# A fused attention, FFN and expert kernel: second products one iteration later, the weight words' intermediate in PSUM, list slots stored without waiting

## The chip, the cores and the metric

The kernel runs on one core of a Trainium2 chip. The metric is the device time of one execution in microseconds (us); a kernel's time is the median over runs. Five engines work side by side and wait for each other through semaphores: PE (TensorE, matrix products), DVE (VectorE), ACT (ScalarE), POOL (GpSimd) and SP (SyncE, which here only issues DMA transfers). Each engine takes its own instructions strictly in order.

## The reference

Three stages follow each other; the second takes the first one's output, the third the second one's.

```
scores = q @ k.T / sqrt(64)                   # 4 batches x 8 heads, 576 x 576
kth    = 32nd largest score of each row
attn   = softmax(scores where scores >= kth)  # the others at -1e9
x      = attn @ v, as 2304 tokens x 512

h = x @ w_in                                  # 512 -> 2048, weights as 8-byte floats
g = maximum(h, 0) + alpha * minimum(h, 0)
x = g @ w_out                                 # 2048 -> 512

logits = x @ w_gate + bias[modality]          # 8 experts
e      = argmax(logits)                       # one expert for each token
out    = softmax(logits)[e] * (relu(x @ w1[e]) @ w2[e])
```

## The kernel before

**Loop.** Attention runs as a software pipeline over 72 iterations (NIT); an iteration takes two tiles of 128 score rows. The order on every engine is the order in which the Python code writes the instructions. In one iteration, for the pair s, DVE finds the 32 largest of each row (L471, L474, L477, L501). PE computes scores for s+1 (L453, L454) and the product with v for s-3 (`av`, L558). ACT copies the scores out of PSUM (L457), makes the mask's operand (L526), the exponentials (L530) and the high half-precision part (L534). POOL subtracts the mask (L527) and makes the low part (L538, L539), and SP issues the transposing DMA PT<-HL (L541).

**FFN within the loop.** As soon as 256 tokens (a chunk) have gone through attention, eight FFN steps for them are fed into the loop, one in an iteration. A step's first product (`mm1`, L637) is issued in one iteration, with a copy by ACT (L651). One iteration later the slope runs on DVE (L665) and the *pair*, that is the high and the low half-precision part of g, on ACT (L672) and POOL (L673). The pair goes into one of GB = 2 buffers named g. In the iteration behind that PE issues the second product (`mm2`, L686), 12 matmuls of 128x512, ahead of the scores and the next `mm1`. PE therefore takes, in an iteration: second product, scores, first product, gate, `av`. The second products of all eight steps add up in two PSUM tiles (psX, two buffers). After the eighth, ACT scales them out (`fin`, L693), PE transposes them back into the same psX (L698), ACT copies these (L700) and PE makes the gate's logits (L704), so the next chunk's first second product waits for L700. What remains behind iteration 72 is done without attention to about 897 us: the *tail*. Then come the experts.

**Weights.** w_in and w_out arrive as 8-byte floats in 32 pieces (L247, 512 KB each, five buffers wraw). `read(x)` turns a piece of 128x512 into f32 by three integer operations on DVE, L259 to L261; their intermediate `t_` is the destination itself, in SBUF: a stretch of Wi or Wo not yet filled, or for the last pieces one of four buffers wlast. ACT and POOL then split the pieces (L266, L271 to L274, L280).

**Lists.** When a chunk's gate is done, `place(r)` writes the tokens' numbers and weights into the experts' lists in DRAM with an indirect DMA on POOL (mapD<-tg,si, L773), with a small memset ahead of it (L772). Only the second place of a chunk is told that it doesn't depend on the first one; all others wait until the earlier places have landed. A block of an expert reads its list back (L1446 for a Block, L1309 for a Unit).

**Stores.** `store()` scales an expert's results into a tile o and writes them out; o has its own buffers in the pools A and B.

Of the kernel before, what the change touches and what calls it, by code (L numbers as in the profile page):

```python
# [8 lines left out]
F32 = mybir.dt.float32  # L9
# [3 lines left out]
I32 = mybir.dt.int32  # L13
I64 = mybir.dt.int64
AF = mybir.ActivationFunctionType
ALU = mybir.AluOpType
# [5 lines left out]
NT, DM, DFF = B * S, H * D, 2048  # L22
E, FE = 8, 1024
KTOP = 32
NCC, NFB = DM // 128, DFF // 128
# [9 lines left out]
LCON = [("late", 1), ("late", 3), ("late", 5)]  # L35
SBUFS = 4
LOOK = 1
GB, GR = 2, 4
ZA, ZN = 1, 1
BIG = 2.0 ** 126  # L40
WBUF = 5
# [19 lines left out]
def tile_kernel(ctx, tc, q, k, v, w_in, w_out, alpha, mod_id, w_gate, mod_bias, w1, w2, out, dbg=None, force=False):  # L61
    nc = tc.nc
    V, A, G, T, SY = nc.vector, nc.scalar, nc.gpsimd, nc.tensor, nc.sync
# [11 lines left out]
    psX = ctx.enter_context(tc.tile_pool(name="psX", bufs=2, space=PSUM))  # L75
# [102 lines left out]
    def phase1(exact, ph, rc, rs, flags, ohs, mp):  # L178
# [51 lines left out]
        def all_weights(words, stage):  # L230
# [20 lines left out]
            def read(x):  # L251

                w_, i = divmod(x, 16)
                f32[x] = W[w_][:, (i + WG) * n:(i + WG + 1) * n] if i + WG < 16 else \
                    stage.tile([128, n], F32, name="wlast", bufs=WG)
                r3 = raws.pop(x).bitcast(I32).rearrange("p (n w) -> p n w", w=2)
                lo, hi = r3[:, :, 0], r3[:, :, 1]
                t_ = f32[x].bitcast(I32)
                V.tensor_scalar(t_, hi, 5, 2, op0=ALU.logical_shift_left, op1=ALU.logical_shift_right)  # L259
                V.scalar_tensor_tensor(t_, hi, -1073741824, t_, op0=ALU.bitwise_and, op1=ALU.bitwise_or)  # L260
                V.scalar_tensor_tensor(t_, lo, 29, t_, op0=ALU.logical_shift_right, op1=ALU.bitwise_or)  # L261

            def square(x):
                w_, i = divmod(x, 16)
# [331 lines left out]
        def chunk(ci, xn, rs):  # L596
# [174 lines left out]
            def place(r):  # L771
                G.memset(spacer, 0.0)  # L772
                d_ = G.indirect_dma_start(out=mapD, out_offset=bass.IndirectOffsetOnAxis(ap=c.si[:, r:r + 1], axis=0),  # L773
                                          in_=c.tg[:, r, :], in_offset=None)
                if r:
                    tc.declare_no_dep(d_.ins, c.placed.ins, reason="other slots")
                c.placed = d_
                state.placed += 1

            def keep():  # L780
# [105 lines left out]
        wgroup = all_weights(words, stage)  # L886
        state.ffn = state.out = None
        state.started = state.placed = 0
        state.alone = False

        def wstep(n):
# [51 lines left out]
        def first_block(s_):  # L943
# [51 lines left out]
            def start():  # L995
                assert state.placed == NTILE - 2
                mp.b0 = Block(0, blk0[0:1, 0:1], blk0[0:1, 1:2], mp)
                for fp in range(4):
                    mp.b0.load(fp)

# [54 lines left out]
        while True:  # L1055
# [44 lines left out]
            for c, fp in post:  # L1100
                for f in c.slope(fp):
                    f()
            for c, fp in paired:
                if c.k == NCH and fp == c.n - 1:
                    mp.b0.mm(0, (0,))
                c.mm2(fp)
                if fp == c.n - 1:
                    c.fin()
                    at("mid", s_, lambda c=c, s_=s_: c.after(s_))
                    at("late", s_, c.keep)  # L1110
            del paired[:]
            for c, fp in post:
                c.pair(fp)
                paired.append((c, fp))
            nxt = []
            if s_ + LOOK < NIT:
                nxt = live[s_ + LOOK] = tile_pair(s_ + LOOK)
# [183 lines left out]
    class Unit:  # L1301


        def __init__(self, i, R, ie, ip, mp):
            self.i, self.R, self.mp = i, R, mp
            self.e = SY.value_load(ie, min_val=0, max_val=E - 1)
            pos = SY.value_load(ip, min_val=0, max_val=E * CAP)
            self.ids = small.tile([128, 4, 2], I32, name="ids4")
            SY.dma_start(self.ids[:, :R], mapD[bass.ds(pos, 128 * R), :].rearrange("(p r) o -> p r o", r=R))  # L1309
            self.raw, self.wp, self.gs = {}, {}, {}  # L1310

        def gather(self):
# [68 lines left out]
                             start=(j == 0 and n == 0), stop=(j == 7 and n == 2))  # L1381

        def store(self):
            o = [p_.tile([128, 2, DM], F32, name="o") for p_ in (self.mp.A, self.mp.B)]
            past = []
            for r in range(self.R):
                A.activation(o[r // 2][:, r % 2, :], self.Y[r], AF.Copy, scale=self.ids.bitcast(F32)[:, r, 1:2])  # L1387
                G.memset(spacer, 0.0)
                d_ = G.indirect_dma_start(out=out, out_offset=bass.IndirectOffsetOnAxis(ap=self.ids[:, r, 0:1], axis=0),  # L1389
                                          in_=o[r // 2][:, r % 2, :], in_offset=None)  # L1390
                for f_ in past:
                    tc.declare_no_dep(d_.ins, f_.ins, reason="other rows")
                past.append(d_)

    def moe_phase(nblk, blk, mp):
# [17 lines left out]
        for i in range(1, nblk):  # L1413
# [21 lines left out]
            o.m2(3)  # L1435
            o.store()

    class Block:


        def __init__(self, i, ie, ip, mp):
            self.i, self.mp = i, mp
            self.e = SY.value_load(ie, min_val=0, max_val=E - 1)
            pos = SY.value_load(ip, min_val=0, max_val=E * CAP)
            self.ids = small.tile([128, 2, 2], I32, name="ids")
            SY.dma_start(self.ids, mapD[bass.ds(pos, 256), :].rearrange("(p r) o -> p r o", r=2))  # L1446
            self.raw, self.wp = {}, {}
            self.gs = {}
            self.Y = None
# [73 lines left out]
                                 start=(fp == 0 and fb == 0 and n == 0), stop=(fp == 3 and fb == 1 and n == 2))  # L1523

        def store(self):
            o = self.half().tile([128, 2, DM], F32, name="o")
            for r in range(2):
                A.activation(o[:, r, :], self.Y[r], AF.Copy, scale=self.ids.bitcast(F32)[:, r, 1:2])
                G.memset(spacer, 0.0)
# [36 lines left out]
```

## Time and profile before

| what | value |
| --- | --- |
| runs | 1156.09 us (median of 3; 1155.61 to 1158.4) |
| the profiled execution's own time | 1153.87 us, of which the trace's span is 1152.2 us |
| granted clock of PE, mean | 0.92 of full speed |
| attention's iterations (first L474 at 39.8, last at 777.5 us) | the iteration is about 8.3 us where DVE has no gap |
| tail of the FFN and first block of the experts | to about 930 us |
| experts' units | about 930 to 1152 us |

The profile names an instruction by its line, its engine and output<-inputs. In a timeline a row gives start, duration, the instruction, its shape, and in square brackets how long the engine was idle before it and what ended that. A row of the waits gives the total, the number of waits and the longest. In a row of a time window the numbers in brackets are counts of instructions; the end of the row is the granted clock of PE, the mean busy share of the DMA engines, and GB/s.

### The profile page before, as it was taken

Reading aid. Unit: us, or ns where it says so; the run is one execution under the profiler, and the core shown is the slowest. Engines: PE = TensorE matmul, PEld = TensorE weight load, DVE = VectorE, ACT = ScalarE, POOL = GpSimd, SP = SyncE. Lnnn points to the kernel's source line nnn. Section 1 sums busy time; section 2 is a strip of 40 time slices with the busy share of each in tenths; the row PEclk is TensorE's granted clock in tenths of the full one; section 3 lists DMA queues with packets and bytes.
Section 4 is the critical chain, followed back from the end, with each engine's and each line's share of the span. In section 5 each row is a group of like instructions: output and inputs, shape, how many; then the busy total and the mean of one; then the engine's idle time right before and its main releaser. Section 6 shows DMA issues by size and latency. Waiting matters only on the chain.

```text
span 1152.2 us, 21482 instructions
## 1 busy us (share of the span) xinstructions
PE 845.0 (73%) x7100; PEld 602.6 (52%) x7100; DVE 823.8 (72%) x2813; ACT 755.2 (66%) x1276; POOL 718.0 (62%) x1106
## 2 busy tenths in 40 slices
PE   0202231347869989878787878989998899999995
PEld 0001121234536557455555555667665778888884
DVE  5788878788889999999888879994326343434342
ACT  6466696898987887878888978795324243342441
POOL 4175496899898898888788999897323220230210
PEclk9999565668899999999989999999999999999998
DMA  8969965586788577586778768765104272543320
GB/s 250 251 171 237 263 145 128 137 180 162 165 202 162 107 184 126 106 177 133 147 148 172 158 138 193 155 128 79 19 19 165 86 262 75 183 135 121 129 92 22
DMA packets 297111, 170.22 MB, mean 148 GB/s; under 512 B 245458, under 2 KB 270034, under 8 KB 296988
## 3 DMA queue, kind: packets, MB, share of 16 engines
q1 hardware_dynamic: 293212, 158.24, 59.0%
q0 software_dynamic: 3776, 10.51, 2.5%
q8 instruction: 57, 0.93, 0.4%
q14 instruction: 66, 0.54, 0.2%
HBM read 81.42 MB, written 25.94 MB: 93 GB/s over the span
## 4 chain that ended last, share of the span: by engine, by line
PE 34%; DVE 23%; POOL 15%; ACT 12%; issue 7%; DMA 6%; SPq 3%; ACTq 0%; POOLq 0%
PE psX L1363 9%; PE psS L1380 9%; PE psX L686 6%; DVE X L501 4%; DVE m L477 4%; PE psS L637 4%; POOL HL L538 4%; POOL S L527 4%; DVE F L477 3%; DMA rawk<-in_k_dram 3%; ACT S L530 2%; POOL qk L419 2%; DVE gr L665 2%; ACT HL L534 2%; PE psH L637 2%
## 5 line engine op out<-in xcount | busy, mean ns | idle before, releaser
L686 PE MATMUL psX<-Wo,g 128*128 128x512 f16 x864 | 218.6, 403 | 53.8 <-POOL g L673 39.6
L527 POOL TENSOR_TENSOR S<-u,S 128x576 f32<-128x576 bf16 x144 | 184.5, 1303 | 47.4 <-ACT u L526 47.2
L637 PEld LDWEIGHTS <-Wi 128*128 128x128 f16 x1920 | 170.8, 99 | 45.7 <-DVE gr L665 14.3
L538 POOL TENSOR_TENSOR HL<-S,HL 128x512 f16<-128x512 f32 x144 | 168.2, 1168 | 20.3 <-ACT HL L534 10.5
L453 PE MATMUL psS<-QK 128*128 128x512 f16 (+1 forms) x160 | 63.7, 436 | 142.6 <-DVE B L471 109.4
L637 PE MATMUL psH<-xT,Wi 128*128 128x256 f16 (+1 forms) x1488 | 158.2, 265 | 12.3 <-DVE gr L665 8.5
L686 PEld LDWEIGHTS <-g 128*128 128x128 f16 x864 | 82.9, 103 | 157.1 <-POOL g L673 49.2
L530 ACT ACTIVATE S<-S,bc,nb 128x576 f32<-128x576 f32 x144 | 124.0, 862 | 40.7 <-POOL S L527 40.7
L453 PEld LDWEIGHTS <-QK 128*128 128x128 f16 (+1 forms) x320 | 32.1, 109 | 203.1 <-DVE B L471 59.5
L1389 POOL DMA_INDIRECT out_dram<-o,ids x18 | 19.9, 1106 | 166.8 <-ACT o L1387 164.0
L477 DVE MAX8 m<-X 128x8 f32<-128x160 f32 x432 | 117.6, 314 | 0.0
L673 POOL TENSOR_TENSOR g<-gr,g 128x512 f16<-128x512 f32 x72 | 84.0, 1166 | 52.6 <-ACT g L672 47.3
L526 ACT ACTIVATE u<-S,bc 128x576 bf16<-128x576 f32 x144 | 103.1, 765 | 15.8 <-POOL bc L506 15.8
L1370 DVE SCALAR_TENSOR_TENSOR gl<-psX,gh 128x512 fp32r<-128x512 f32 (+1 forms) x40 | 25.4, 637 | 115.5 <-ACT gh L1369 110.9
L534 ACT ACTIVATE HL<-S 128x576 f16<-128x576 f32 x144 | 91.3, 680 | 12.9 <-DMA PT<-HL 12.7
L1369 ACT ACTIVATE gh<-psX 128x512 fp32r<-128x512 f32 (+1 forms) x40 | 22.3, 557 | 109.7 <-PE psX L1363 107.9
L457 ACT ACTIVATE S<-psS 128x576 f32<-128x576 f32 x144 | 84.1, 633 | 8.6 <-PE psS L454 8.6
L501 DVE MATCH_REPLACE8 X<-m,X 128x160 f32<-128x160 f32 x288 | 87.0, 310 | 0.0
L558 PE MATMUL bankO<-VV,PT 128*128 128x66 f16 (+1 forms) x2240 | 86.0, 200 | 0.0
L558 PEld LDWEIGHTS <-PT 128*128 128x128 f16 (+1 forms) x2240 | 82.3, 105 | 4.8 <-issue 3.5
L474 DVE SCALAR_TENSOR_TENSOR X<-psS,S 128x288 f32<-128x288 f32 (+1 forms) x144 | 80.8, 603 | 2.5
L672 ACT ACTIVATE g<-gr 128x512 f16<-128x512 f32 x72 | 44.9, 623 | 40.5 <-DVE gr L665 24.1
(290 smaller groups left out, 2098.6 us busy)
## 6 DMA issues: line engine op xcount, KB each, us to landing
raw<-in_moe_w_dram SPq DMA_DIRECT2D x40, 512.0 KB
qkD<-QK SPq DMA_DIRECT2D x16, 576.0 KB
QK<-qkD SPq DMA_DIRECT2D x16, 576.0 KB
wraw<-in_moe_w_in_dram SPq DMA_DIRECT2D x16, 512.0 KB
wraw<-in_moe_w_out_dram SPq DMA_DIRECT2D x16, 512.0 KB
vvD<-VV SPq DMA_DIRECT2D x16, 325.0 KB
VV<-vvD SPq DMA_DIRECT2D x16, 325.0 KB
K<-QK SPq DMA_DIRECT2D x32, 144.0 KB
```

The source lines that it names most:

```text
L477: ops.append(lambda: V.max(o, a_))
L501: ops.append(lambda i_=i_, r=r: V.match_replace(out=dst(i_), in_to_replace=m[:, i_, 8 * r:8 * r + 8], in_values=src(i_) if r == 0 else dst ...
L526: A.activation(u, t.S, AF.Relu, scale=-BIG, bias=t.cut)
L527: G.tensor_tensor(t.S, u, t.S, op=ALU.subtract)
L530: A.activation(t.S, t.S, AF.Exp, scale=t.c.negc, bias=t.b)
L534: A.activation(t.HL.rearrange("p a b -> p (a b)")[:, 0:S], t.S, AF.Copy)
L538: G.tensor_tensor(f[:, 640:1152], t.S[:, 0:512], f[:, 0:512], op=ALU.subtract)
L558: T.matmul(oo, l, r, start=(n_ == 0), stop=(n_ == len(ops) - 1), skip_group_check=True)
L637: T.matmul(h[:, fb, :], Wi[:, 4 * cc + f0 // 512, wh, f0 % 512:f0 % 512 + 128], c.xT[:, :R, xh_, cc, :], start=(n == 0), stop=(n == 11))
L686: T.matmul(c.X2[r], g[:, gh, fb, r * 128:r * 128 + 128], Wo[:, FB * fp + fb, wh, :], start=(fp == 0 and fb == 0 and n == 0), stop=(fp == c ...
L1363: T.matmul(h, w_[:, cc, f0:f0 + 128], x_[:, cc, :], start=(n == 0), stop=(n == 11))
L1380: T.matmul(self.Y[r], g_[:, r * 128:r * 128 + 128], w_[:, j % 2, :], start=(j == 0 and n == 0), stop=(j == 7 and n == 2))
```

## The change

1. **Lag.** A pair made in iteration `s_` is noted with the iteration from which its second product may run: `s_ + 2` in place of `s_ + 1`, and still `s_ + 1` where `s_ + 2` would lie behind the last iteration. In the loop the second product comes ahead of the pair of the same iteration, so up to three pairs live: GB is 3. The loop that issues second products stops behind a chunk's last one. A chunk's `fin`, gate, places and its store x2D move with it.
2. **Intermediate in PSUM.** `t_` is a tile of psX; only the third operation writes SBUF. The two psX tiles are not used by anything else while the weights are read.
3. **Places.** Every place is told that it depends on no earlier one, and every reading of a list waits for all places so far (`behind`).
4. **Stores' slots.** o of Block, and of the Unit's first half, takes a buffer of the tile xth in the same pool.

```
-GB, GR = 2, 4
+GB, GR = 3, 4
...
-                t_ = f32[x].bitcast(I32)
+                t_ = psX.tile([128, n], F32, name="psX").bitcast(I32)
                 V.tensor_scalar(t_, hi, 5, 2, op0=ALU.logical_shift_left, op1=ALU.logical_shift_right)
                 V.scalar_tensor_tensor(t_, hi, -1073741824, t_, op0=ALU.bitwise_and, op1=ALU.bitwise_or)
-                V.scalar_tensor_tensor(t_, lo, 29, t_, op0=ALU.logical_shift_right, op1=ALU.bitwise_or)
+                V.scalar_tensor_tensor(f32[x].bitcast(I32), lo, 29, t_, op0=ALU.logical_shift_right, op1=ALU.bitwise_or)
...
-                if r:
-                    tc.declare_no_dep(d_.ins, c.placed.ins, reason="other slots")
-                c.placed = d_
+                for p_ in state.places:
+                    tc.declare_no_dep(d_.ins, p_.ins, reason="other slots")
+                state.places.append(d_)
...
+                mp.places, mp.seen = state.places, 0
+                behind(mp.b0.list, mp)
...
-            for c, fp in paired:
+            last = False
+            while paired and paired[0][0] <= s_ and not last:
+                _, c, fp = paired.pop(0)
+                last = fp == c.n - 1
                 if c.k == NCH and fp == c.n - 1:
                     mp.b0.mm(0, (0,))
                 c.mm2(fp)
...
-            del paired[:]
             for c, fp in post:
                 c.pair(fp)
-                paired.append((c, fp))
+                paired.append((s_ + (2 if s_ + 2 < NIT else 1), c, fp))
...
-            SY.dma_start(self.ids[:, :R], mapD[bass.ds(pos, 128 * R), :].rearrange("(p r) o -> p r o", r=R))
+            behind(SY.dma_start(self.ids[:, :R], mapD[bass.ds(pos, 128 * R), :].rearrange("(p r) o -> p r o", r=R)), mp)
...
-            o = [p_.tile([128, 2, DM], F32, name="o") for p_ in (self.mp.A, self.mp.B)]
+            o = [self.mp.A.tile([128, NCC, 256], F32, name="xth").rearrange("p (r a) t -> p r (a t)", r=2),
+                 self.mp.B.tile([128, 2, DM], F32, name="o")]
...
+    def behind(list_, mp):
+        for p_ in mp.places[mp.seen:]:
+            tc.add_manual_dep(list_.ins, p_.ins.name, mybir.DependencyInfo(
+                mybir.DependencyClass.Sync, mybir.DependencyReason.DATA), reason="all that was placed")
+        mp.seen = len(mp.places)
...
-            SY.dma_start(self.ids, mapD[bass.ds(pos, 256), :].rearrange("(p r) o -> p r o", r=2))
+            self.list = SY.dma_start(self.ids, mapD[bass.ds(pos, 256), :].rearrange("(p r) o -> p r o", r=2))
+            if i:
+                behind(self.list, mp)
...
-            o = self.half().tile([128, 2, DM], F32, name="o")
+            o = self.half().tile([128, NCC, 256], F32, name="xth").rearrange("p (r a) t -> p r (a t)", r=2)
```

The first place is DVE at one of the pieces that go into the buffers wlast. Before:

```order
L259 TENSOR_SCALAR wlast<-wraw 128x512 [waits DMAHW0_49,Pool_49]
L260 SCALAR_TENSOR_TENSOR wlast<-wraw,wlast 128x512 [waits DVE_49]
L261 SCALAR_TENSOR_TENSOR wlast<-wraw,wlast 128x512 [waits DVE_49]
L259 TENSOR_SCALAR wlast<-wraw 128x512 [waits DMAHW1_49]
L260 SCALAR_TENSOR_TENSOR wlast<-wraw,wlast 128x512 [waits DVE_49]
L261 SCALAR_TENSOR_TENSOR wlast<-wraw,wlast 128x512 [waits DVE_49]
```

And after:

```order
L259 TENSOR_SCALAR psX<-wraw 128x512 [waits DMAHW0_49]
L260 SCALAR_TENSOR_TENSOR psX<-wraw,psX 128x512 [waits DVE_49]
L261 SCALAR_TENSOR_TENSOR wlast<-wraw,psX 128x512 [waits DVE_49,Pool_49]
L259 TENSOR_SCALAR psX<-wraw 128x512 [waits DMAHW1_49]
L260 SCALAR_TENSOR_TENSOR psX<-wraw,psX 128x512 [waits DVE_49]
L261 SCALAR_TENSOR_TENSOR wlast<-wraw,psX 128x512 [waits DVE_49]
```

The number of operations stays; two of three write PSUM, and the wait for POOL, which frees the buffer wlast, has moved from the first to the third.

The second place is ACT at the end of attention, where a chunk's sums come out of the loop (x<-psX is L693, gr<-psX is L700; the last L457 belongs to the last iteration's scores). Before:

```order
L526 ACTIVATE u<-S,bc 128x576 x2
L693 ACTIVATE x_11062<-psX,un 128x512 x2
L672 ACTIVATE g<-gr 128x512
L530 ACTIVATE S<-S,bc,nb_8261 128x576
L457 ACTIVATE S<-psS 128x576 x2
L530 ACTIVATE S<-S,bc,nb_8261 128x576
L651 ACTIVATE gr<-psH 128x512
L534 ACTIVATE HL<-S 128x576 x2
L700 ACTIVATE gr<-psX 128x512 x2
L526 ACTIVATE u<-S,bc 128x576 x2
```

And after:

```order
L526 ACTIVATE u<-S,bc 128x576 x2
L672 ACTIVATE g<-gr 128x512
L530 ACTIVATE S<-S,bc,nb_8277 128x576
L457 ACTIVATE S<-psS 128x576 x2
L530 ACTIVATE S<-S,bc,nb_8277 128x576
L651 ACTIVATE gr<-psH 128x512
L534 ACTIVATE HL<-S 128x576 x2
L526 ACTIVATE u<-S,bc 128x576 x2
L693 ACTIVATE x_11245<-psX,un 128x512 x2
L672 ACTIVATE g<-gr 128x512
L530 ACTIVATE S<-S,bc,nb_8627 128x576 x2
L651 ACTIVATE gr<-psH 128x512
```

Both copies stand one iteration later: L693 behind the last L457, and L700 (the second row behind these, after L534) behind the next iteration's exponentials.

The third place is POOL in the tail, at three places in a row (tg and si, the numbers with their weights and the slots, come from DVE). Before:

```order
L745 COPY tg<-tok 128x2 [waits DMASW4_49,DMASW3_49]
L772 MEMSET spacer 1x1
L773 DMA mapD<-tg,si 18944x2
L772 MEMSET spacer 1x1 [waits Pool_49]
L773 DMA mapD<-tg,si 18944x2 [waits DMASW5_49,DVE_49]
L772 MEMSET spacer 1x1 [waits Pool_49]
L773 DMA mapD<-tg,si 18944x2
L673 TENSOR_TENSOR g<-gr,g 128x512 [waits Activation_49]
```

And after:

```order
L745 COPY tg<-tok 128x2 [waits DMASW4_49,DMASW3_49]
L772 MEMSET spacer 1x1
L773 DMA mapD<-tg,si 18944x2
L772 MEMSET spacer 1x1 [waits Pool_49]
L773 DMA mapD<-tg,si 18944x2 [waits DVE_49]
L772 MEMSET spacer 1x1 [waits Pool_49]
L773 DMA mapD<-tg,si 18944x2
L673 TENSOR_TENSOR g<-gr,g 128x512 [waits Activation_49]
```

The order is the same; the middle place has lost its wait for POOL's own earlier DMA (DMASW5) and keeps the one for DVE.

## Rows read from the trace of the kernel before

**Rows 1.** The page's part 1: busy time, share of the span, instructions.

```profile
PE 845.0 (73%) x7100; PEld 602.6 (52%) x7100; DVE 823.8 (72%) x2813; ACT 755.2 (66%) x1276; POOL 718.0 (62%) x1106
```

**Rows 2.** Time windows: busy time of PE, PEld, DVE, ACT, POOL, then clock, DMA.

```profile
400.00:450.00 50.00, 45.33 (x493) 31.10 (x490) 49.37 (x198) 38.37 (x62) 45.24 (x66) 1.00 0.69 142
...
950.00:1000.00 50.00, 50.00 (x226) 40.81 (x226) 17.83 (x22) 17.02 (x25) 9.08 (x12) 1.00 0.39 128
```

**Rows 3.** DVE's groups by shape, 0 to 250 us; then lines L259, L261: min/median/max ns.

```profile
L261 DVE SCALAR_TENSOR_TENSOR wlast<-wraw,wlast 128x512 int32<-128x512 int32 x8 | 10.4, 1300 | 0.3
...
L259 DVE TENSOR_SCALAR Wo<-wraw 128x512 int32<-128x512 int32 x12 | 7.0, 586 | 3.9 <-DMA wraw<-in_moe_w_out_dram 3.9
...
L259 DVE TENSOR_SCALAR Wi<-wraw x12: 411/420/1505, 9.3 to 55.6; 128x512 int32<-128x512 int32 x12
...
L261 DVE SCALAR_TENSOR_TENSOR Wi<-wraw,Wi x12: 691/692/1646, 10.5 to 56.8; 128x512 int32<-128x512 int32 x12
```

**Rows 4.** Timeline around 20 us, one instruction each of DVE and POOL.

```profile
20.53 1.65 DVE L261 SCALAR_TENSOR_TENSOR Wi<-wraw,Wi 128x512 int32<-128x512 int32 x1
...
19.91 1.72 POOL L419 TENSOR_TENSOR qk<-rawk,qk 128x576 f16<-128x576 f32 x1
```

**Rows 5.** Lines L474 and L1370, DVE with a PSUM operand: min/median/max ns.

```profile
L474 DVE SCALAR_TENSOR_TENSOR X<-psS,S x144: 457/602/749, 40.3 to 777.5; 128x288 f32<-128x288 f32 x72, 128x576 f32<-128x576 f32 x72
...
L1370 DVE SCALAR_TENSOR_TENSOR gl<-psX,gh x40: 408/692/693, 935.0 to 1136.1; 128x512 fp32r<-128x512 f32 x32, 128x256 fp32r<-128x256 f32 x8
```

**Rows 6.** Timelines of DVE, then of POOL, 179 to 202 us.

```profile
179.55 1.36 DVE L259 TENSOR_SCALAR wlast<-wraw 128x512 int32<-128x512 int32 x1 [3.06 <-POOL Wi L280]
180.95 1.67 DVE L260 SCALAR_TENSOR_TENSOR wlast<-wraw,wlast 128x512 int32<-128x512 int32 x1
...
193.70 0.46 DVE L474 SCALAR_TENSOR_TENSOR psS<-psS,S 128x288 f32<-128x288 f32 x1
...
201.78 0.20 POOL L506 TENSOR_TENSOR bc<-m,nb 128x4 f32<-128x4 f32 x1 [10.34 <-DVE wp1k L212]
```

**Rows 7.** Timelines of DVE, then of SP, 55 to 78 us.

```profile
55.61 0.41 DVE L259 TENSOR_SCALAR Wi<-wraw 128x512 int32<-128x512 int32 x1
...
68.10 0.46 DVE L474 SCALAR_TENSOR_TENSOR psS<-psS,S 128x288 f32<-128x288 f32 x1
...
77.57 2.00 SPq L247 DMA_DIRECT2D wraw<-in_moe_w_out_dram  x4
```

**Rows 8.** Waits by engine and line: three of 237 to 350 us, two of 562 to 710 us.

```profile
PE psX L686 <- POOL g L673: 14.8, 5, 5.2
...
ACT gr L651 <- PE psH L637: 1.4, 2, 0.7
...
SPq L541 <- PE bankO L558: 2.6, 1, 2.6
...
PE psX L686 <- POOL g L673: 18.1, 6, 4.9
...
SPq L541 <- PE bankO L558: 3.7, 3, 1.5
```

**Rows 9.** End of attention: timelines of PE and ACT, and the chain that ended last.

```profile
779.30 2.75 PE L686 MATMUL psX<-Wo,g 128*128 128x512 f16 x12 [2.79 <-ACT gr L700]
...
785.26 1.48 ACT L534 ACTIVATE HL<-S 128x576 f16<-128x576 f32 x2
...
806.28 2.59 PE psX L686 x12
```

**Rows 10.** Tail, 860 to 868 us: timelines of POOL, DVE and PE.

```profile
860.17 0.98 POOL L773 DMA_INDIRECT mapD<-tg,si  x1 [0.42 <-issue]
...
864.57 0.97 POOL L773 DMA_INDIRECT mapD<-tg,si  x1 [3.32 <-DVE mx L975]
...
860.22 0.17 DVE L769 RECIPROCAL tg<-sm 128x2 f32<-128x2 f32 x1
...
868.05 2.33 PE L686 MATMUL psX<-Wo,g 128*128 128x512 f16 x10 [3.28 <-POOL g L673]
```

More of the change, by code (lines that the diff above doesn't have):

```diff
@@ L888, in phase1 @@
         state.started = state.placed = 0
+        state.places = []
         state.alone = False
```

## The prediction

> **What bounds the kernel now.** I began with the busy shares of the page [rows 1]: PE 73%, DVE 72%, ACT 66%, POOL 62%, so no engine bounds the whole. The time windows say why [rows 2]. Between 400 and 450 us DVE is busy 49.37 of 50 us: attention in its even stretches hangs on DVE. Between 950 and 1000 us PE is busy 50.00 of 50 us: the experts, and most of the tail before them, hang on PE. Whatever the change does to PE, POOL or ACT inside an even stretch of attention is therefore worth nothing there; it can pay only where DVE has gaps: at the start (to about 240 us, while the weights are read), in the stretches at 237 to 350 and 562 to 710 us, and at the end. So I went on with DVE's groups in the first 250 us, the timelines where weights are read, the waits in the two uneven stretches, the chain of waits at the end of attention, and the places in the tail. DVE's groups show the three operations of a read [rows 3]: nine groups for three destinations, 96 instructions, 80.8 us together, of which the first is 10.4 us (1.30 us each) and the last 7.0 us (0.59 us each).
>
> **Part 1, the intermediate in PSUM.** Nothing is removed: 96 instructions stay 96. What may change is how long one takes. In SBUF an undisturbed L259 takes 0.42 us and an undisturbed L260 or L261 0.69 us, but some take up to 1.5 and 1.65 us [rows 3]. The long ones fall on POOL's long ones: POOL's L419 ran 1.72 us from 19.91, and DVE's L261 1.65 us from 20.53 [rows 4]; the two engines alternate there. With a PSUM operand DVE is not stretched, with POOL busy beside it all through attention: L474's 144 instructions have a maximum of 0.749 us, and L1370, the same kind of operation on 128x512, takes 0.692 us with a maximum of 0.693 [rows 5]. No row shows these three integer operations on PSUM; I price each at 0.69 us, the nearest row in shape. For L259 that is worse than its 0.42 us undisturbed. The bounds: 0.42 us for L259 as before, and above, the 0.84 us at which 96 of them take the 80.8 us of now. At 0.69 us they take 66.4 us: 14.4 us less DVE work, net of what L259 loses.
>
> Against the change speaks the Trainium skill, "VectorE: DVE Perf Modes", section "Why PSUM operands drop a tier": a PSUM operand takes the doubled rate from a 4-byte operation. By that page's formula for PSUM sources (its section on the TRN2 errata) one operation would be an estimated 658 ns, so 63.2 us for the 96 where the rows give 66.4. No row before shows L259 on PSUM.
>
> How much of the 14.4 us lies on the path? Three places.
>
> At 179.55 us four reads run back to back until 193.70 us, 14.15 us, the first after an idle of 3.06 us in which it waited for POOL to free the buffer wlast [rows 6]. In the changed order this wait stands at the third operation, so the first two run in that idle. The other ten take 6.9 us. The reads would end at about 186.4 us, 7.3 us earlier. POOL waits for what DVE does next: it stood 10.34 us until 201.78 us for the maxima that DVE makes behind the reads [rows 6]; with 7.3 us less it still waits 3, so the whole 7.3 us is on the path. ACT and SP, which hang on POOL here, move along.
>
> At 55.61 us four reads take until 68.10 us, 12.5 us [rows 7]; at 0.69 us each 8.3, so 4.2 us less. But the next words are only issued by SP at 77.57 us, 9.5 us behind the last read [rows 7], by a queue that holds other waits. I pass on 1.5 us, between 0 and 4.2.
>
> The rest of the 14.4 us (5.9 us of it is the first place's busy time, 4.2 the second's) is 4.3 us, scattered over stretches in which DVE also waits for the words to arrive (the last of the nine groups shows 3.9 us of that [rows 3]). I count it at nothing: the transfers cover it; without that cover it gains up to 4.3.
>
> Sum of part 1: **-8.8 us**, between -3 (half the first place, no second) and -15.8.
>
> **Part 2, the lag inside attention.** In the two uneven stretches PE waits 14.8 and 18.1 us at L686 for POOL's g, 32.9 us in all [rows 8]. With the pair a whole iteration older that wait should go. But a waiting PE costs only what waits for PE. There ACT waits 1.4 us for the first products, and SP 2.6 and 3.7 us at L541 for the products with v [rows 8]: 7.7 us. Half of it I take as on the path, since POOL and ACT, the other engines of the loop, are late next: **-4 us**, between 0 and -10 (just under a third of the 32.9). In DVE's even stretches it is 0. The third buffer costs only room. SP's store x2D of each chunk comes an iteration later, behind that iteration's loads and transposes; nobody reads it before the experts, and its place would cost only if it delayed L541, by the half microsecond of an issue (four took 2.00 us [rows 7]).
>
> **Part 3, the lag at the end of attention.** PE falls idle here, then becomes the bound: at 779.30 us it has waited 2.79 us for L700 and from then on it does not rest; the tail is a chain of second products of 2.59 us each and first products [rows 9]. With the lag, one second product more is left when attention ends: +2.6 us, if PE then works without a gap. The chunk's boundary moves into the next iteration too: L700 comes behind that iteration's L534 (785.26 to 786.7 us) [rows 9], so with the two copies at about 787.8 us. PE does the older second product in place of waiting from 776.5 us; with that, the next first product (2.6 us each) and under 2.3 us of transposes and products with v it runs dry between 783 and 784. It waits some 4 us there in place of 2.79, and then catches up with two second products in a row: 2.6 + 4 - 2.8 = 3.8. So **+4 us**, between +2.6 and +4.7 (dry at 783).
>
> **Part 4, places.** All waits of L773 are short but one, in the tail. The place at 860.17 us was issued; the next at 864.57 us came after 3.32 us of idle; the row names a DVE operation, but the pairs and slots of that chunk were ready at about 860.4 us (L769 at 860.22) [rows 10]. What the order shows as taken away there, POOL's wait for its own earlier DMA, is the one that fits. Without it the three places and the pair behind them are done at about 864.7 us, and PE, which stood 3.28 us until 868.05 us for that pair [rows 10], need not wait. The tail hangs on PE, so **-3.3 us**, and 0 if it was DVE after all. The lists' readings wait for all places as before: 0. The stores' buffers change owner, and their former readers (first products) are long done: 0.
>
> **Sum:** -8.8 - 4 + 4 - 3.3 = -12.1 us. Against the profiled execution's 1153.87 us that is 1141.8; its own time lies 2.2 us under the median of the runs, so against 1156.09 it is **1144 us**. A measurement here tells about 0.3% (3.5 us) from no change: faster means below 1152.6, slower above 1159.6.
>
> **Rivals.** *The lag opens the whole loop* (chance 0.16). The chain in the uneven stretches goes from POOL's g through PE to ACT and back to POOL; if each wait of PE holds back the next iteration, half of the 32.9 us comes back, -16.5 in place of -4, and the time is 1156.1 - 24.6 = 1131.5. For it: five of those waits are nearly 5 us each [rows 8]. Against: the direct waits for PE are 7.7 us.
>
> *The gains are hidden* (0.15). The words, not DVE, set the start, and POOL's 10.34 us wait shrinks only until ACT's scores are late; part 1 is -3, part 2 is 0, with +4 and -3.3 the time is 1156.1 - 2.3 = 1153.8. For it: the idle times before L259 are put down to the words. Against: at 179 us all words have arrived, the wait there is for POOL.
>
> *The change doesn't shorten the reads* (in the next case): if an operation between SBUF and PSUM is stretched by POOL as before, or takes over 0.84 us, part 1 is 0. Against: the maxima in rows 5; but L261 still reads and writes SBUF besides PSUM.
>
> *The end of attention costs more than the rest gives* (0.07). The backlog of part 3 is paid for certain, 4.7 us at its upper bound, where PE has no idle left to take it up in. If part 1 fails as above, part 2 is 0 and the place waits for DVE, the time is 1160.8, slower. It decides from the point where parts 1, 2 and 4 together give less than 1.2 us. Against: part 1 alone has 7.3 us at one place with a visible waiter.
>
> **How the numbers follow.** Forecast 0.62 (all of it faster), open loop 0.16 (faster), hidden 0.15 (0.04 faster, 0.11 same), end of attention 0.07 (0.06 slower, 0.01 same): faster 0.82, same 0.12, slower 0.06. The range runs from the open loop's 1132 to 1153, just short of the hidden case: part 1's bounds with part 2's give 1156.1 - 15.8 - 10 + 2.6 - 3.3 = 1129.6 and 1156.1 - 3 + 0 + 4.7 - 3.3 = 1154.5, and both at once are unlikely.
>
> **What would show it.** Right: L259 to L261 all near 0.69 us with maxima below 0.8; the reads that began at 179.55 end 7 us sooner, and POOL's wait behind them is about 3 us; L686's waits for g in the two stretches fall from 32.9 us to a few; at the end one iteration with 24 L686 in a row and PE some 4 us later than the rest; the three places in the tail about 1.2 us apart, with no wait of PE behind them. Wrong: reads still stretched to 1.6 us (part 1 falls); PE's waits gone but the stretches as long as before (part 2 is 0); PE's waits at L686 replaced by waits of ACT for PE (the lag has moved the gap), or 3.3 us still between two places (part 4).

## The result, and the profile after

The changed kernel takes 1142.01 us (median of 4 runs, 1140.67 to 1144.57) against 1156.03 us: a ratio of 0.9877, 95% interval 0.9855 to 0.9899, 14 us less. 1144 us had been forecast, with a range of 1132 to 1153. Its profiled execution took 1141.56 us, with a span of 1139.7 us.

The page's first part, and then the two time windows that answer [rows 2]:

```profile
PE 842.4 (74%) x7100; PEld 605.6 (53%) x7100; DVE 802.1 (70%) x2814; ACT 755.7 (66%) x1276; POOL 704.7 (62%) x1105
```

```profile
400.00:450.00 50.00, 46.33 (x491) 32.51 (x492) 49.49 (x204) 39.88 (x65) 43.80 (x67) 1.00 0.68 139
...
950.00:1000.00 50.00, 50.00 (x227) 40.94 (x226) 18.28 (x23) 17.96 (x26) 9.07 (x12) 1.00 0.39 127
```

Against [rows 1] DVE lost 21.7 us of work, 14.7 of it in the reads (80.8 to 66.1 us), and POOL 13.3; the bounds are the same as before, DVE in attention's even stretch and PE in the experts. Where the time went shows best when the two traces are laid over each other. Each iteration of attention begins on DVE with the first L474. The table takes its start in the changed kernel minus the one before, and the same for some matmuls of PE behind attention; all are worked out from the timelines.

| place | after minus before, us | change since the line above |
| --- | --- | --- |
| iteration 8 (167 us) | -1.47 | -1.47 |
| iteration 9 (194 us) | -8.77 | -7.30 |
| iteration 13 (237 us) | -8.92 | -0.15 |
| iteration 49 (562 us) | -13.29 | -4.37 |
| iteration 62 (700 us) | -15.65 | -2.36 |
| iteration 71, the last (777 us) | -11.51 | +4.14 |
| tail, first L704 of a whole chunk (850 us) | -7.00 | +4.51 |
| tail, that chunk's L740 (859 us) | -8.69 | -1.69 |
| tail, the L637 behind the places (870 us) | -11.80 | -3.11 |
| end of the span (1152 us) | -12.5 | -0.7 |

The rows behind the steps from 13 on: the first L474 of iterations 13, 49, 62 and 71 and the L704 at 850 us, before; then the same after.

```profile
237.43 0.47 DVE L474 SCALAR_TENSOR_TENSOR psS<-psS,S 128x288 f32<-128x288 f32 x1 [2.13 <-ACT S L457]
...
562.38 0.45 DVE L474 SCALAR_TENSOR_TENSOR psS<-psS,S 128x288 f32<-128x288 f32 x1
...
700.15 0.47 DVE L474 SCALAR_TENSOR_TENSOR psS<-psS,S 128x288 f32<-128x288 f32 x1 [0.25 <-ACT S L457]
...
776.63 0.45 DVE L474 SCALAR_TENSOR_TENSOR psS<-psS,S 128x288 f32<-128x288 f32 x1
...
850.12 1.95 PE L704 MATMUL bankO<-wg,gr 128*128 128x8 f32 x16 [0.30 <-ACT gr L700]
```

```profile
228.51 0.47 DVE L474 SCALAR_TENSOR_TENSOR psS<-psS,S 128x288 f32<-128x288 f32 x1 [2.13 <-ACT S L457]
...
549.09 0.45 DVE L474 SCALAR_TENSOR_TENSOR psS<-psS,S 128x288 f32<-128x288 f32 x1
...
684.50 0.47 DVE L474 SCALAR_TENSOR_TENSOR psS<-psS,S 128x288 f32<-128x288 f32 x1 [0.67 <-ACT S L457]
...
765.12 0.47 DVE L474 SCALAR_TENSOR_TENSOR psS<-psS,S 128x288 f32<-128x288 f32 x1
...
843.12 1.95 PE L704 MATMUL bankO<-wg,gr 128*128 128x8 f32 x16 [0.31 <-ACT gr L700]
```

Reads: lines L259 and L261 of the changed kernel (min/median/max ns, first and last start), then DVE and POOL around 180 us; they answer [rows 3, 5, 6].

```profile
L259 DVE TENSOR_SCALAR psX<-wraw x32: 672/685/695, 10.0 to 182.9; 128x512 int32<-128x512 int32 x32
...
L261 DVE SCALAR_TENSOR_TENSOR wlast<-wraw,psX x8: 686/686/689, 59.3 to 184.3; 128x512 int32<-128x512 int32 x8
```

```profile
174.95 0.68 DVE L259 TENSOR_SCALAR psX<-wraw 128x512 int32<-128x512 int32 x1
175.67 0.69 DVE L260 SCALAR_TENSOR_TENSOR psX<-wraw,psX 128x512 int32<-128x512 int32 x1
178.09 0.69 DVE L261 SCALAR_TENSOR_TENSOR wlast<-wraw,psX 128x512 int32<-128x512 int32 x1 [1.73 <-POOL Wi L280]
...
184.93 0.46 DVE L474 SCALAR_TENSOR_TENSOR psS<-psS,S 128x288 f32<-128x288 f32 x1
...
193.01 0.20 POOL L506 TENSOR_TENSOR bc<-m,nb 128x4 f32<-128x4 f32 x1 [4.91 <-DVE wp1k L212]
```

No read is stretched any more. The first two operations run ahead of POOL's release, and the reads end 8.8 us earlier than before, 7.3 of them won here. POOL waits 4.91 us in place of 10.34; about 3 had been expected, but POOL itself is done earlier too, since its operations beside the reads are shorter (the L419 of 1.72 us takes 1.27 here).

Laid beside POOL's timeline, the 96 operations of before fall in two. The 43 with no POOL operation beside them took at most 0.427 us (L259) and 0.693 us (L260, L261), so every stretched one had POOL beside it. In the changed kernel 54 have POOL beside them, and none takes more than 0.697 us.

Waits in the two uneven stretches (228 to 338 and 549 to 697 us here): the waits of PE at L686 for POOL's g, 14.8 and 18.1 us before [rows 8], have no row left. What stands there now, from each stretch one row of the engines and, last, one of SP's queue:

```profile
PE psS L453 <- DVE B L471: 16.3, 5, 7.1
...
ACT HL L534 <- DMA PT<-HL: 9.0, 7, 2.8
...
SPq L541 <- PE bankO L558: 2.4, 1, 2.4
```

Before, the second of these rows was, from 562 to 710 us:

```profile
ACT HL L534 <- DMA PT<-HL: 4.7, 5, 2.2
```

The end of attention and the tail, PE's and POOL's timelines; they answer [rows 9, 10].

```profile
769.42 2.85 PE L637 MATMUL psH<-xT,Wi 128*128 128x128 f16 x48 [2.71 <-DVE gr L665]
...
776.11 5.34 PE L686 MATMUL psX<-Wo,g 128*128 128x512 f16 x24 [2.09 <-ACT gr L700]
...
851.49 0.98 POOL L773 DMA_INDIRECT mapD<-tg,si  x1 [0.42 <-issue]
...
852.77 0.97 POOL L773 DMA_INDIRECT mapD<-tg,si  x1 [0.21 <-issue]
...
854.04 0.97 POOL L773 DMA_INDIRECT mapD<-tg,si  x1 [0.22 <-issue]
...
856.26 2.33 PE L686 MATMUL psX<-Wo,g 128*128 128x512 f16 x10 [0.17 <-POOL g L673]
```

The 24 L686 in a row are there. Three places follow each other by 1.28 us, and PE's wait of 3.28 us is 0.17.

### The profile page after: what moved, and what is told of

It is laid out like the page before. It is cut to its first block, busy times and chain, and to the rows that moved or that the text cites. A ratio compares the mean times of both kernels' runs of the same rounds, so it can differ in the third digit from the quotient of the medians.

```text
span 1139.7 us, 21483 instructions
## 1 busy us (share of the span) xinstructions
PE 842.4 (74%) x7100; PEld 605.6 (53%) x7100; DVE 802.1 (70%) x2814; ACT 755.7 (66%) x1276; POOL 704.7 (62%) x1105
## 4 chain that ended last, share of the span: by engine, by line
PE 31%; POOL 17%; DVE 17%; ACT 15%; issue 8%; DMA 7%; SPq 3%; ACTq 0%; POOLq 0%
PE psS L1385 9%; PE psX L1368 8%; PE psX L686 5%; POOL S L527 5%; POOL HL L538 4%; PE psS L637 4%; DVE X L501 3%; DVE m L477 3%; DVE F L477 2%; ACT S L530 2%; DMA rawk<-in_k_dram 2%; DMA PT<-HL 2%; ACT u L526 2%; ACT HL L534 2%; POOL g L673 2%
## 5 line engine op out<-in xcount | busy, mean ns | idle before, releaser
L686 PE MATMUL psX<-Wo,g 128*128 128x512 f16 x864 | 203.8, 387 | 9.8 <-ACT gr L700 9.6
L637 PEld LDWEIGHTS <-Wi 128*128 128x128 f16 x1920 | 175.2, 101 | 56.0 <-DVE gr L665 21.6
L637 PE MATMUL psH<-xT,Wi 128*128 128x256 f16 (+1 forms) x1488 | 167.1, 273 | 17.8 <-DVE gr L665 11.4
L686 PEld LDWEIGHTS <-g 128*128 128x128 f16 x864 | 82.1, 100 | 100.3 <-issue 17.0
L1395 POOL DMA_INDIRECT out_dram<-xth,ids x10 | 9.9, 993 | 164.0 <-ACT xth L1393 162.9
L534 ACT ACTIVATE HL<-S 128x576 f16<-128x576 f32 x144 | 91.7, 681 | 18.6 <-DMA PT<-HL 18.4
L457 ACT ACTIVATE S<-psS 128x576 f32<-128x576 f32 x144 | 84.2, 634 | 7.5 <-PE psS L454 7.5
L474 DVE SCALAR_TENSOR_TENSOR X<-psS,S 128x288 f32<-128x288 f32 (+1 forms) x144 | 80.7, 602 | 2.5
```

Of the source, the lines that this page charges most:

```text
L534: A.activation(t.HL.rearrange("p a b -> p (a b)")[:, 0:S], t.S, AF.Copy)
L637: T.matmul(h[:, fb, :], Wi[:, 4 * cc + f0 // 512, wh, f0 % 512:f0 % 512 + 128], c.xT[:, :R, xh_, cc, :], start=(n == 0), stop=(n == 11))
L686: T.matmul(c.X2[r], g[:, gh, fb, r * 128:r * 128 + 128], Wo[:, FB * fp + fb, wh, :], start=(fp == 0 and fb == 0 and n == 0), stop=(fp == c ...
```

## The experiments

All kernels are set beside runs of the kernel before, 1156.1 to 1156.6 us. Beside a median stands its range: some kernels spread over 4 to 11 us, so their steps are read from the overlaid traces, and the medians second.

**The intermediate in PSUM alone.** The kernel before with

```
-                t_ = f32[x].bitcast(I32)
+                t_ = psX.tile([128, n], F32, name="psX").bitcast(I32)
```

and the third operation writing `f32[x]`.

> The kernel before with one edit: the reads' intermediate lies in PSUM. Theory: the three operations take 0.69 us each, and what that gives is fixed by two places, the four reads at 180 us (7.3 us) and the four at 56 us (1.5 us). The ninth iteration's first L474 starts 8.8 us earlier than before, nothing after it gives that back, and the time is 1156 - 9 = 1147 us (1145 to 1149). Rival: the start's gain is used up later by the loop (POOL, ACT) as long as PE's waits for g stay; the iterations of 500 us would then start less than 5 us earlier and the time is 1151 to 1156 us.

1147.65 us (1146.40 to 1148.40), ratio 0.9926 (0.9911 to 0.9941): -8.5 us. The step from iteration 8 to 9 is -7.29 us, iteration 13 stands at -8.73 and iteration 49 at -8.46. The gain lasts through the even stretches with PE's waits still in place; 2.4 us of it are lost between 49 and 71.

**All but the intermediate.** The changed kernel with `t_` in its destination again.

> The changed kernel with the intermediate back in its destination in SBUF. Theory: the 8.9 us of the start are lost and nothing else moves, 1151 us (1149 to 1153). Rival: part of the start's gain is lost later in any case (the changed kernel loses 3.3 us at one iteration around 690 us), so taking it away costs less: 1146 to 1148 us.

1151.81 us (1149.58 to 1152.35), as expected: 9.8 us above the changed kernel. Its iteration 9 stands at +0.35 us, and two of the three steps behind that are the same as in the changed kernel (-4.32 from 13 to 49, +4.08 from 62 to 71; from 49 to 62 it is -0.74). So the loss at 62 to 71 isn't the price of the faster start.

**A scratch tile in SBUF.** The changed kernel with

```
-                t_ = psX.tile([128, n], F32, name="psX").bitcast(I32)
+                t_ = words.tile([128, n], F32, name="wtmp", bufs=2).bitcast(I32)
```

> The changed kernel with the intermediate in a tile of its own in SBUF (two buffers) in place of PSUM. The wait for the buffer wlast stands at the third operation as in the changed kernel; the operations work on SBUF alone as before. Theory: most of the gain is that operations with a PSUM operand are not stretched beside POOL; here they still reach 1.6 us, the reads at 180 us win only what runs in the idle ahead, 1.4 to 3 us, and the time is 1147 to 1150 us. Rival: the moved wait is what counts: 1142 to 1144 us.

1150.92 us (1147.78 to 1155.35), a little above the range expected: the step from iteration 8 to 9 is -0.65 us in place of -7.30, where 1.4 to 3 us had been given to the moved wait. DVE and POOL at the reads around 185 us:

```profile
179.94 1.63 DVE L261 SCALAR_TENSOR_TENSOR wlast<-wraw,wtmp 128x512 int32<-128x512 int32 x1 [2.66 <-POOL Wi L280]
...
189.35 1.79 DVE L260 SCALAR_TENSOR_TENSOR wtmp<-wraw,wtmp 128x512 int32<-128x512 int32 x1
...
192.75 0.45 DVE L474 SCALAR_TENSOR_TENSOR psS<-psS,S 128x288 f32<-128x288 f32 x1
...
200.82 0.20 POOL L506 TENSOR_TENSOR bc<-m,nb 128x4 f32<-128x4 f32 x1 [8.55 <-DVE wp1k L212]
```

The wait stands at the third operation, and two operations run ahead of it; the others are stretched to 1.6 and 1.8 us as before. The moved wait by itself is worth almost nothing; PSUM is what counts.

**PSUM for the wlast pieces alone.** `t_` in PSUM only `if i + WG >= 16`, else in its destination.

> The changed kernel with the intermediate in PSUM for the eight pieces of the buffers wlast alone; the 24 that go to Wi and Wo have it in their destination as before. Theory: only the reads with a visible waiter count, and seven of the eight that stand at 56 and 180 us are wlast pieces: within 1 us of the changed kernel, 1142 us (1141 to 1143.5). Rival: every stretched read costs (the other pieces' excess over 0.69 us is about 5 us less what L259 loses): 1144 to 1146 us.

1146.29 us (1138.58 to 1147.40), above the range expected and the rival's. But the step from iteration 8 to 9 is -7.29 us, with 8 of 32 pieces in PSUM. It starts 0.9 us late at iteration 0, and iteration 8 stands at +0.90. Two kernels with all pieces in PSUM have as much there (+0.45 without lag, +0.36 with the places as before) while others have -1.5, so the median doesn't tell what the other 24 pieces give. Counted from iteration 0, the ten kernels with all pieces in PSUM win 0.37 to 2.16 us up to iteration 8 and this one wins nothing: that much lies in the 24.

**Places as before.** The changed kernel with the dependences of L773 restored.

> The changed kernel with the places' dependences as before. Theory: the middle one of the three places in the tail again waits some 3.3 us for the one ahead to land, PE waits for the pair behind it, and the time is 3.1 us more, 1145 us (1144 to 1146.5). Rival: the wait in the kernel before was for DVE's operation that its row names, and the places' dependences are worth nothing: 1142 us.

1147.27 us (1141.55 to 1149.68), above the range expected. POOL and PE in the tail:

```profile
855.94 0.98 POOL L773 DMA_INDIRECT mapD<-tg,si  x1 [0.42 <-issue]
...
860.73 0.97 POOL L773 DMA_INDIRECT mapD<-tg,si  x1 [3.72 <-DVE ge L978]
...
864.21 2.33 PE L686 MATMUL psX<-Wo,g 128*128 128x512 f16 x10 [3.67 <-POOL g L673]
```

The wait is back with nothing but the dependence changed, and the step over the places is +0.39 us in place of -3.11, so 3.5 us. The row names another DVE operation than before, one that ended at about the time: a wait for two semaphores is put down to the one that shows. The medians are 5 us apart; what else lies between them isn't shown. The profiled run is this kernel's slowest, with iteration 13 at -6.84 in place of -8.92.

**All but the lag.** `paired.append((s_ + 1, c, fp))`, three buffers g stay.

> The changed kernel with the second product again one iteration behind its pair (three buffers g stay). Theory from the two traces: the lag gave 2.6 us inside attention and took 4.5 us at its end, so without it the time is about 2 us less, 1140 us (1138 to 1142). Rival: the lag is worth the 4 us and more that PE's waits suggested and the end costs nothing that would not be lost anyway; then the time is 1146 us or more.

1144.05 us (1139.95 to 1146.46), 2 us above the changed kernel, with overlapping ranges: neither the theory nor the rival. By the trace, from iteration 13 to 49 it gains 0.36 us where the lag gave 4.37, from 62 to 71 it loses nothing, and to the first L704 in the tail it loses 2.14, of which about 1.5 is a stretch of PE at half the clock (12 matmuls of L686 in 4.29 us in place of 2.75).

**The lag ends eight iterations earlier.** `s_ + 2 < NIT - 8` in place of `s_ + 2 < NIT`.

> The changed kernel, but the second products go back to one iteration behind the pair eight iterations earlier, so that the two second products in a row fall into the even stretch where DVE is the bound and PE has some 10% to spare. Theory: the 4.5 us at the end of attention are an effect of the backlog there; they go, the even stretch hides the additional second product, and the time is 1137.5 us (1136 to 1140). Rival: PE is late for one iteration in the even stretch and ACT and POOL hand that on to DVE; then the cost only moves, 1141 to 1144 us.

1143.46 us (1140.66 to 1146.04). The rival holds. The cost from iteration 71 to the tail's L704 falls from 4.51 to 2.20 us, of which about 1.5 is the same stretch at half the clock as without the lag. But the loop loses 5.18 us between 62 and 71, 4.74 of it from 64 to 67, where the second products come two in a row (the changed kernel loses 4.14 between 62 and 71, 3.31 of it at iteration 63). PE's timeline in the iteration with two second products, and then the waits from 700 to 720 us:

```profile
707.50 6.78 PE L686 MATMUL psX<-Wo,g 128*128 128x512 f16 x24 [2.86 <-ACT gr L700]
```

```profile
ACT S L457 <- PE psS L454: 3.8, 1, 3.8
DVE psS L474 <- ACT S L457: 3.1, 1, 3.1
```

The 24 matmuls begin late, behind L700, and take 6.78 us, where 24 take 5.34 at the end of the changed kernel's attention (the clock granted from 707 to 711 us is 0.57 of full speed); the scores behind them come late, ACT waits 3.8 us for these and DVE 3.1 for ACT. In a stretch where DVE is the bound, that cost is paid in full.

**The lag for a part of the chunks.** `2 if c.k < 4 else 1`, and `2 if c.k >= 4 and s_ + 2 < NIT else 1`.

> The changed kernel with the lag for the FFN chunks 0 to 3 alone (second products up to iteration 51); later chunks run their second products one iteration behind the pair, as before. Theory from the traces so far: the lag gives 4.2 us between iterations 13 and 49 and takes back about that much at iterations 62 to 67 and a little in the tail; with the lag in the first part alone the gain stays: iteration 71 starts 4 us earlier against iteration 13, and the time is 4 us under the kernel without any lag, 1140 us (1138 to 1142). Rival: what was gained early is lost at 62 to 67 in any case, since the transfers there set the pace: 1144 us as without lag.

> The changed kernel with the lag for the FFN chunks from the fifth on alone. Theory: nothing changes between iterations 13 and 49, some 2 us are lost between 49 and 71 and under 1 us net in the tail, so this is the slowest of the lag's parts: 1146.5 us (1144.5 to 1148). Rival: the loss at 62 to 67 came only because the lag's earlier gain had moved the loop against the transfers; then nothing is lost here: 1142 to 1144 us.

The early part alone: 1146.91 us (1141.98 to 1151.70); the late part alone: 1145.31 us (1142.37 to 1149.31). The early part's theory fell, by its time too; the late part's time is in its range, but the 2 us it was to lose between 49 and 71 are not lost. The early lag gives its 4.31 us from 13 to 49, and the profiled run then loses 4.82 us to iteration 62 and 6.21 to 71, without any lag there. The late lag loses nothing in these stretches (+0.23 and +0.03). So the loss behind iteration 62 isn't made by the lag that runs there; it shows in the kernels whose early chunks lag. The first 4.8 us fit the run above: where the lag ends, at iteration 52, two second products (24 L686) fall into one iteration. How the early lag brings on the later loss isn't shown. Being ahead in time doesn't do it: at iteration 62 the early part alone stands at -8.00 us and then loses 6.21, and the late part alone at -8.53 and loses nothing.

**A third buffer for HL.** `name="HL", bufs=3`, with the lag as changed; then with the lag for the chunks 0 to 3 alone, and with no lag.

> The changed kernel with a third buffer for HL, the tile that ACT writes and the transposing transfer reads. Theory: the 3.3 us lost at iteration 63 are ACT's waits at L534 for the transposes to release their tile (5.1 us of waits there); with a third tile they go, and the time is 1138.5 us (1137 to 1140.5). Rival: the transposes themselves are late and the next reader (the products with v) or the queue of SP waits in ACT's place: 1141 to 1143 us.

> Both edits: the lag for the chunks 0 to 3 alone and a third buffer for HL. Theory: the lag's late part is where the waits for the transposes arise, so with it gone the third buffer adds little: 1139 us (1137 to 1141), within 1.5 us of the kernel with the lag for the chunks 0 to 3 alone. Rival: the transposes hold up ACT in other places too (9.5 us of such waits in the two uneven stretches of the changed kernel), and the two edits add up to 1136 us or less.

> The changed kernel without any lag (second products one iteration behind the pair) but with a third buffer for HL. Theory: the lag's gain of some 4 us between iterations 13 and 49 is its own, its loss at iteration 63 is ACT's wait for HL; once the third buffer has taken that wait away the lag is worth 4 us less about 0.7 in the tail, so without it the time is 3 us above the kernel with lag and third buffer, 1142.5 us (1141 to 1144). Rival: the third buffer's 3 us come in both cases and the lag's gain is lost somewhere else behind iteration 49 anyway: 1139 to 1140.5 us.

What led to it: the timelines of ACT and DVE at iteration 62 to 63 of the changed kernel, and a piece of its chain of waits there (start, duration, what):

```profile
688.53 0.68 ACT L534 ACTIVATE HL<-S 128x576 f16<-128x576 f32 x1 [2.83 <-DMA PT<-HL]
691.09 0.68 ACT L534 ACTIVATE HL<-S 128x576 f16<-128x576 f32 x1 [1.88 <-DMA PT<-HL]
...
696.58 0.47 DVE L474 SCALAR_TENSOR_TENSOR psS<-psS,S 128x288 f32<-128x288 f32 x1 [3.30 <-ACT S L457]
```

```profile
681.59 9.42 DMA PT<-HL
```

The second transposing transfer of iteration 61 took 9.4 us of the chain; ACT could not write HL and came late with the scores. With a third HL, ACT's rows in the same iterations are

```profile
677.67 1.25 ACT L534 ACTIVATE HL<-S 128x576 f16<-128x576 f32 x2
686.19 1.25 ACT L534 ACTIVATE HL<-S 128x576 f16<-128x576 f32 x2
694.54 1.25 ACT L534 ACTIVATE HL<-S 128x576 f16<-128x576 f32 x2
```

without a wait, and the time is 1139.14 us (1137.16 to 1141.98), ratio 0.9860 (0.9836 to 0.9884), as expected. Iteration 63 loses nothing; 2.09 us are still lost between 62 and 71. With the lag in the chunks 0 to 3 alone it is 1139.02 us (1134.92 to 1145.93), ratio 0.9846 (0.9821 to 0.9870), the time expected but 7.9 us below the same kernel with two HL, where under 1.5 had been said; the profiled run is its slowest and loses 4.72 us from 49 to 62, where the lag ends, as above, and 4.28 more from 62 to 71, in spite of the third buffer. Without lag it is 1141.17 us (1137.30 to 1141.79), near the theory. By the medians the third buffer gives 2.9 us with and without lag, and the lag 2.0 us with and without the third buffer; but these ranges overlap two by two, and in the traces without lag the third buffer gains 0.5 us between iterations 13 and 71 (-0.83 in place of -0.32), so the 2.9 us there aren't shown to be the buffer's. By their medians the two kernels with lag and a third HL are 3 us below the changed one, though the intervals of the ratios overlap.

One sign goes with the loss in all the traces. SP issues the two transposes of iteration 61 behind the loads of QK and K. In the nine kernels whose early chunks lag, they come 0.16 us behind the last load (L355), the second one's issue takes 4.0 to 6.3 us (2.62 in the kernel with lag throughout and a third HL), and 2.1 to 6.2 us are lost from 62 to 71. In the other five they come 0.97 to 1.28 us behind, the second takes 1.6 to 2.8 us, and at most 1.7 us are lost (all against the kernel before, which is one of the five). The second issue in the changed kernel, and then in the one with the late lag alone:

```profile
681.59 5.86 SPq L541 DMA_TRANSPOSE PT<-HL  x1
```

```profile
688.65 1.62 SPq L541 DMA_TRANSPOSE PT<-HL  x1
```

That the transposes run late because they come close behind the loads is not shown by a run of its own.

## Why the prediction was right, step by step

**Part 1 (-8.8 us) was right in mechanism and size.** The 96 operations were priced at 66.4 us and take 66.1; the trace shows -8.9 at iteration 13, from the very places: -7.30 at the four reads at 180 us, in every kernel that has PSUM there, and -1.47 left at iteration 8 of the 4.13 us that iteration 2 first won. The price of 0.69 us for L259, taken from the nearest row in shape, is 0.685. The Trainium skill's page formula ("VectorE: DVE Perf Modes", the section on the TRN2 errata) gave an estimated 658 ns; the trace has medians of 685 to 695 (L259, with its source in SBUF and only its result in PSUM, has 685 in place of 420), so the rule of the lost doubled rate agrees, and the measured price stands. What the forecast left open is why PSUM helps. The traces say: with all operands in SBUF an operation waits for POOL's, with one in PSUM it does not, even if it writes SBUF (L261, at most 0.689 us). The Trainium skill ("SBUF — State Buffer", section "SBUF: two separate sides") has the rule: GpSimd and a DVE operation that has two SBUF inputs (against a GpSimd operation that reads SBUF) or runs in a two-port mode take a shared port pair exclusively, and the later one blocks until the first has ended. L260 at 1.79 us in the scratch tile's run agrees, and so do POOL's shorter operations in the changed kernel. L259 has one SBUF input and was stretched as well (1.36 us at 179.55 us); that it runs in a two-port mode is not shown by a trace.

**Part 2 (-4 us) was right to iteration 49 and too large behind it.** From 13 to 49 the lag gives 4.37 us, and without it 0.36. PE's 14.8 us of waits in that stretch are gone and bought 4 us, about what the others' waits for PE there had said (1.4 and 2.6 us), not half of it. But from 49 to 71 the sum is +1.8 us: 2.36 us won to iteration 62 are given back with 4.14. The step that failed is "half of it I take as on the path" for the second stretch; there ACT's waits for the transposes stood next, 4.7 us before and 9.0 us now. Part 2 is -2.6 us. That these waits carry the 3.31 us at iteration 63 is shown in the changed kernel by the third HL buffer, with which that step is gone. It isn't the whole: 2.09 us of the 4.14 stay with it, and 4.28 with the lag in the early chunks alone. Why the transposes are late in the kernels whose early chunks lag, and not in others that stand as early or earlier (-8.53 with the late lag alone, -9.93 without lag and with a third HL), stays open. Nor is the stretch behind 49 the same in all kernels without lag: PSUM alone loses 2.38 us there, the others nothing.

**Part 3 (+4 us) was right in size.** The trace shows +4.51; five other kernels with the lag at the end and two HL have +4.16 to +4.42, and the kernel with PSUM alone +0.02. The mechanism holds in its sum and not in its place: one wait of some 4 us for L700 had been expected, and PE has two, 2.71 us for the first product's gr (L665) and 2.09 for L700. With the additional second product that is 2.6 + 4.8 - 2.8 = 4.6. It was not seen that the clock would give something back: 1.69 us, below.

**Part 4 (-3.3 us) was right.** It is -3.11, and the dependence alone brings the wait back.

**The sum.** -8.9 - 2.6 + 4.5 - 3.1 = -10.1; with the clock's -1.7 and 0.7 in the units, -12.5 against the -12.1 forecast. That the sum is so near owes something to chance: part 2 gave 1.4 us less, and the clock, which no term had, gave 1.7. The 1144 us had 2.2 us added for the profiled run of before, which lies under the median; the medians differ by 14.0 us. No run takes the stores' slots back by themselves, so what the 0.7 us are is not shown.

**Of the rivals**, the open loop fell: PE's waits vanished and 4 us came. The hidden start fell with the step of 7.30 us, and with it the reads that PSUM would not shorten. The end of attention cost its price, but parts 1 and 4 paid for it.

## What to carry to other kernels

Before an engine's operations are moved or cut, look whether their maximum stands far above their median, and what runs beside the long ones: here some two thirds of the gain came from where an intermediate lies, with the same number of operations. A wait that is large and has no waiter of its own (PE's 32.9 us) is worth about what others wait for that engine, not its length; and a gain inside a pipelined loop is safe only as far as the next shared resource, here the transfer that frees a tile. A shift in a software pipeline has to be paid where it ends: two steps in one iteration, at the end or wherever the shift is taken back, and taking it back inside the loop cost as much as at the end (4.74 against 4.51 us, though 1.4 of the first are a stretch at a lower clock).

## What the runs showed of the hardware

**The clock in the tail.** Windows of 6 us behind the L704 at 850 us (843 after), before and then after (the third number from the end is the granted clock):

```profile
850.00:856.00 6.00, 5.88 (x28) 3.39 (x29) 3.06 (x12) 1.18 (x3) 1.15 (x1) 0.72 0.01 3
```

```profile
843.00:849.00 6.00, 5.88 (x42) 4.31 (x43) 3.05 (x12) 1.18 (x3) 1.19 (x1) 1.00 0.01 3
```

PE is busy for the same 5.88 us, at a granted clock of 0.72 and of 1.00; in windows of 2 us the clock of before is 0.50 (1.2 of 2.4 GHz) at 854 us. PE had run without a gap over 0.31 us for 50 us before either. The drop costs 1.7 us here. At this place it shows in six profiles (before, PSUM alone, and four without the lag at the end) and not in eight (all with the lag at the end, and the one without lag but with a third HL). So it goes mostly, not always, with the order at the end of attention; what sets it off is open. Other drops to half the clock lie elsewhere in every profile, so the 1.69 us are this place's and not a count of all.

**Spread.** The changed kernels' runs lie up to 11 us apart. The overlaid profiles of kernels with all pieces in PSUM differ by up to 3.4 us at iteration 8 (-2.92 to +0.45) and by whole stalls of 1.5 to 4 us at a few iterations behind 49. So single medians of kernels that differ by 3 us don't rank them; the same step read in several traces (-7.29 to -7.31 in eleven kernels) does.
